# A graph tensor product by sorted buckets: 4.5 instead of 5 slot tiles a bucket in the first of three parts

## The chip, the cores and the metric

The kernel runs on one core of a Trainium2 chip. Its engines work side by side, each in the order of its own queue: PE (matrix products; its weight loads are listed as PEld), DVE (VectorE), ACT (ScalarE), POOL (GpSimd, which here issues the indirect DMAs) and SP (SyncE, which issues the plain DMAs). The metric is device time in microseconds (us), the median of several runs; less is better.

## The reference

A graph has N = 10000 nodes and E = 640000 edges, each with a random source and a random destination. Every node carries 64 channels of 4 numbers, every edge 4 numbers Y and 4 edge features.

```python
np.random.seed(seed)                                   # seed = 0
src = np.random.randint(0, N, size=E); dst = np.random.randint(0, N, size=E)
...
R = silu(edge_feat @ w_rad)                            # (E, 64)
xs = x[src]                                            # (E, 64, 4)
tp = einsum('eci,ef,ifo->eco', xs, Y, cg)
agg = segment_sum(R[:, :, None] * tp, dst, N)          # sum over the edges into a node
out = einsum('ncm,cd->ndm', agg, w_mix)
```

So for each edge a row of x is gathered, scaled per channel by R, combined with Y, and added to its destination. The constant combination with `cg` and `w_mix` is linear and comes last, after the sum over edges.

## The kernel before

**Tiles and parts.** 128 edges are a tile, and E is 5000 tiles. `SPLIT` (L35) cuts them into three parts: 0.3, 0.355 and 0.345 of the tiles (1488, 1776 and 1736). Each part is sorted by destination in two passes and then summed up.

**First sort** (`pass1`, L703). The nodes form 20 groups. Chunks of up to 24 tiles (16 in the first part) are routed so that the edges of a group lie together in the memory array `grp`. PE does the routing with one-hot matrices (L650), which ACT and DVE build (L623, L635, L639); POOL writes each chunk to memory with one indirect DMA (L669). The first part's first sort, and the second sort of its first group, run before any messages; the first sorts of parts two and three are woven into the messages of the part before.

**Second sort** (`pass2`, L804). The groups of a part are sorted the same way into buckets of up to 32 nodes, 15 or 16 to a group and 313 in all, in the memory array `bkt`. Each bucket there has a fixed row of slots: `BT = 17` tiles of 128, of which part k owns `SPLIT[k][1]` (5, 6, 6). Within a bucket a running counter says where the next edge goes. When a part begins, the counter is raised to the first slot of that part (`kc` in `front`, L821), so slots that the part before left free stay empty; when a part has more edges than slots, they run on into the next part's slots. Only the end of the whole row is a limit: a chunk's piece of a bucket that would cross it is sent whole to a spill list behind `bkt` (`tables`, L471: `over`, `sc`, `kov`). A piece has 8 rows of S slots, S being what a chunk can need at most: 35 for a chunk of up to 24 tiles, 12 for the short chunk of 6 tiles that closes each group of the last part.

**Messages** (`messages`, L894). A unit is one bucket in one part. `load_bucket` (L376) brings the slots of a whole group into `pay` with 8 DMAs on SP, one for each of the 8 rows in which a bucket's slots are interleaved. `index` (L915) splits the keys into source and destination. `gather` (L938) issues one indirect DMA on POOL for each tile, 128 rows of x into a buffer `xg` with room for 7 units. `rests`, `spell`, `turn`, `turned`, `radial` and `silu` make R; `products` (L1017, DVE, L1021) multiplies it into `xg`; `spots` (L1005, DVE, L1011 and L1014) makes S, which holds Y in the column of the edge's node within the bucket and zero elsewhere; `sums` (L1023, PE, L1032) adds up `xg` times S over the unit's tiles in one PSUM tile G; `evict` (L1048) takes it out and adds the earlier parts' sum, read back from memory (`fetch`, L1041). In the last part the result is mixed (L1080) and stored (L1092).

The order on PE, DVE and ACT is written out: each step of the loop runs the stages of `quarters` for unit k plus a lead, 5 units for the gathers, 8 for the index, 1 for the products, 0 for the sums. `groups` (L1118) weaves in the two sorts by counts of steps. POOL's and SP's instructions stand in program order on their queues.

**The end** (`overflow`, L1194). After the last unit a loop works off the spill lists, first that of the first sort, then that of the second. A pass takes 5 tiles (`OT`): it loads them (L1241), gathers their rows of x (L1262), computes them directly, and for one tile after the other reads the output rows that it touches (L1281), adds (L1316) and writes them back (L1317). The number of passes is computed on the chip from the length of the list. At last the count of edges seen is compared with E; if it differs, the output is cleared and all edges are done over in the same kind of loop (L1229).

Of the kernel before, what the change touches and what calls it, by code (L numbers as in the profile page):

```python
# [18 lines left out]
F = mybir.dt.float32  # L19
BF = mybir.dt.bfloat16  # L20
I32 = mybir.dt.int32
# [4 lines left out]
P = 128  # L26
# [6 lines left out]
BT = 17  # L33
UT = 6
SPLIT = ((0.3, (5,)), (0.355, (6,)), (0.345, (6,)))  # L35
# [68 lines left out]
class Kernel:  # L104
    def __init__(self, ctx, tc, x, src, dst, Y, ef, w_rad, cg, w_mix, out):
# [18 lines left out]
        assert N <= 1 << 14 and BT == sum(sum(u) for _, u in SPLIT)  # L124
# [27 lines left out]
        for _, u in SPLIT:  # L152
            self.btile.append(self.btile[-1] + sum(u))
# [6 lines left out]
        p.stride = BT * P // p.R + p.S  # L160
# [214 lines left out]

    def load_bucket(self, pay, k, g):  # L376

        p, u = self.p2, sum(SPLIT[k][1])
        nb, o = self.nb(g), g * MB * p.R * p.stride * W
        rows = p.dst.rearrange("s w -> (s w)")[o:o + nb * p.R * p.stride * W].rearrange("(b r q) -> r b q", b=nb, r=p.R)  # L380
        s = P // p.R
        a, z = (t * s * W for t in (self.btile[k], self.btile[k + 1]))
        for r in range(p.R):
            self.nc.sync.dma_start(pay[r * s:(r + 1) * s, :nb, :],
                                   rows[r][:, a:z].rearrange("b (p q) -> p b q", p=s))
# [418 lines left out]
    def pass2(self):  # L804
# [44 lines left out]
        for i, (k, g) in enumerate(self.segs):  # L849
            sizes = self.sizes2(k, g)  # L850
            off = [0] + list(itertools.accumulate(sizes))
            if i not in ready:
                yield from front(i, loads(i) if i % self.NG else [load(k, g)])
            D, Wt, tab, c0 = ready.pop(i)

            side = None
            if i and i + 1 < len(self.segs) and self.segs[i + 1][0] == k and i + 1 not in ready:
                side = front(i + 1, loads(i + 1))
            for said in self.route(ps, lambda c: (D[:, off[c]:off[c + 1]], Wt[:, off[c]:off[c + 1]]), sizes,
                                   lambda c: (tab, c0 + c)):  # L860
                if said == "held":
                    if self.held == ps.key:
                        side = self.go(side)[0]
                    yield said
                    continue
                yield max(said - 1, 1)
                if side is not None:
                    side, at = self.go(side)
                    if at == "held":
                        yield at  # L870
                yield 1
            while side is not None:
                side, at = self.go(side)
                yield at
            n = sum(SPLIT[k][1])
            pay = ph.tile([P, MB * max(sum(u) for _, u in SPLIT) * W], F, name="pay")
            pay = pay[:, :MB * n * W].rearrange("p (b q) -> p b q", b=MB)
            self.load_bucket(pay, k, g)
            self.pay[k, g] = pay
            yield  # L880
# [13 lines left out]
    def messages(self):  # L894

        nc, ph = self.nc, self.ph
        units = [((k, g), j, s) for k, g in self.segs for j in range(self.nb(g)) for s in range(len(SPLIT[k][1]))]
        MT = max(sum(u) for _, u in SPLIT)
# [3 lines left out]
        def quad(k):  # L902

            (p, g), j, s = units[k]
            n0, b, nb = self.grp[g]
            j -= j % 4
            return [(n0 + i * b, min(b, self.N - n0 - i * b)) for i in range(j, min(j + 4, nb))]

        def tiles(k):

            g, j, s = units[k]
            u = SPLIT[g[0]][1]
            return sum(u[:s]), u[s]

        def index(k):  # L915

            g, j, s = units[k]
            if s or j:
                return
            m = self.nb(g[1])  # L920
            ut = sum(SPLIT[g[0]][1])
            key = self.pay[g].rearrange("p b (t w) -> p b t w", w=W)[:, :m, :, 0].bitcast(I32)
            si = ph.tile([P, MB, MT], I32, name="sidx", bufs=2)
            nc.vector.tensor_scalar(si[:, :m, :ut], key, (1 << 14) - 1, None, op0=OP.bitwise_and)
            di = ph.tile([P, MB, MT], I32, name="didx", bufs=2)
            nc.vector.tensor_scalar(di[:, :m, :ut], key, 14, None, op0=OP.logical_shift_right)
            dl = ph.tile([P, MB, MT], F, name="dlc", bufs=2)
            n0, b, _ = self.grp[g[1]]
            nc.vector.tensor_scalar(dl[:, :m, :ut], di[:, :m, :ut], float(TD), None, op0=OP.is_ge)
            got = ph.tile([P, 1], F, name="got")  # L930
            nc.vector.tensor_reduce(got, dl[:, :m, :ut], axis=AX.XY, op=OP.add)
            nc.vector.tensor_tensor(self.seen, self.seen, got, op=OP.add)
            nc.vector.scalar_tensor_tensor(dl[:, :m, :ut], di[:, :m, :ut], -float(TD + n0),
                                           self.bn[b][:, :m].unsqueeze(2).to_broadcast([P, m, ut]),
                                           op0=OP.add, op1=OP.subtract)
            IDX[g] = (si, dl)

        def gather(k):  # L938
            g, j, s = units[k]
            si, t0, ut = IDX[g][0][:, j, :], *tiles(k)  # L940
            xg = XG[k] = ph.tile([P, UT, 256], F, name="xg", bufs=LG + 2)
            for t in range(ut):
                u = t0 + t
                nc.gpsimd.indirect_dma_start(  # L944
                    out=xg[:, t, :], out_offset=None, in_=self.x,
                    in_offset=bass.IndirectOffsetOnAxis(ap=si[:, u:u + 1], axis=0))

        def payload(k):
            g, j, s = units[k]
            t0, ut = tiles(k)  # L950
            return self.pay[g][:, j, t0 * W:(t0 + ut) * W], ut

        def rests(k):
            g, j, s = units[k]
            if j % EB:
                return
            ut = tiles(k)[1]
            b = min(EB, self.nb(g[1]) - j)
            ef = self.pay[g][:, j:j + b].rearrange("p b (t w) -> p (b t) w", w=W)[:, :, 5:9]
            top = lambda t: t.bitcast(BF).rearrange("p t (f h) -> p t f h", h=2)[:, :, :, 1]  # L960
            r = ph.tile([P, 2, EB * UT, 4], F, name="rest", bufs=1)
            n = b * ut
            nc.vector.tensor_tensor(r[:, 0, :n], ef, top(ef), op=OP.subtract)
            nc.vector.tensor_tensor(r[:, 1, :n], r[:, 0, :n], top(r[:, 0, :n]), op=OP.subtract)
            EP[k] = [top(ef), top(r[:, 0, :n]), top(r[:, 1, :n])]

        def spell(k):
            g, j, s = units[k]
            if j % EB:
                return  # L970
            E = ph.tile([P, EB * UT * 36], BF, name="E")
            if tiles(k)[1] < UT:
                n = EP[k][0].shape[1] * 36
                nc.vector.memset(E[:, n:n + 36], 0.0)
# [4 lines left out]
            for i in range(min(EB, self.nb(g[1]) - j)):  # L979
                EQ[k + i] = (E, i * tiles(k)[1] * 36)  # L980
# [12 lines left out]
        def radial(k):  # L993
            ut = payload(k)[1]
# [10 lines left out]
        def spots(k):  # L1005
            g, j, s = units[k]
            pb, ut = payload(k)
            pb = pb.rearrange("p (t w) -> p t w", w=W)
            t0 = tiles(k)[0]
            dl = IDX[g][1][:, j, t0:t0 + ut]  # L1010
# [4 lines left out]
                                    pb[:, :, 1:5].unsqueeze(2).to_broadcast([P, ut, NB, 4]), op=OP.mult)  # L1015

        def products(k):  # L1017
            ut = payload(k)[1]
# [4 lines left out]
        def sums(k):  # L1023
            g, j, s = units[k]
            ut = tiles(k)[1]
            if s == 0:
                GP[g, j] = self.ps.tile([P, 2, NB, 4], F, name="G", tag="G", bufs=1)
            G = GP[g, j]
            V, S = VS.pop(k), SS.pop(k)
            for t in range(ut):  # L1030
                for h in range(2):
                    nc.tensor.matmul(G[:, h].rearrange("p n f -> p (n f)"),  # L1032
                                     V[:, t, 32 * h:32 * h + 32, :].rearrange("p c i -> p (c i)"),
                                     S[:, t].rearrange("p n f -> p (n f)"),
                                     start=(s + t + h == 0), stop=(last(k) and t == ut - 1),
                                     skip_group_check=True)

        def last(k):
            return units[k][2] == len(SPLIT[units[k][0][0]][1]) - 1

        def fetch(k):  # L1041

            g, j, s = units[k]
            if g[0] and s == 0:
# [3 lines left out]
        def evict(k):  # L1048
            g, j, s = units[k]
            if not last(k):  # L1050
                return
# [15 lines left out]
        def full(k):  # L1067
            g, j, s = units[k]
            if g[0] == len(SPLIT) - 1 and last(k) and (j % 4 == 3 or j == self.nb(g[1]) - 1):
# [3 lines left out]
        def mix(k):  # L1073
            g, j, s = units[k]
# [9 lines left out]
        def mixed(k, po):  # L1084
            g, j, s = units[k]
# [32 lines left out]
    def groups(self):  # L1118
# [5 lines left out]
        for k, g in segs:  # L1124
            u += self.nb(g) * len(SPLIT[k][1])
# [263 lines left out]
```

## Time and profile before

| | |
|---|---|
| median of 3 runs | 8055.66 us (8052.32 to 8060.37) |
| profiled execution, its own time: the span | 9825.7 us |
| busy PE, weight loads, DVE, ACT, POOL | 74%, 68%, 66%, 40%, 59% of the span |
| indirect DMAs on POOL: gathers, first sort, second sort | 5321, 240, 260 |
| routing matmuls (L650), matmuls of the sums (L1032) | 20530, 21284 |

A float32 matmul appears as two instructions with two weight loads. Rows of the profile name the line, the engine, the operation, the tile written and the tiles read; `x5` is a count. An indirect DMA's time on POOL is the time to issue it, not that of its data. In a row's brackets stands how long the engine was idle before the instruction and what released it. "Remote" means that the releasing event is not among the recorded instructions, "issue" that nothing recorded was waited for. The profiled execution is longer than the others because it is being recorded.

### The profile page before, as it was taken

The numbers are of one execution on the slowest core, as the hardware profiler recorded it, in microseconds if no ns is written. First come the engines' busy times: TensorE is split into PE (matmuls) and PEld (weight loads), VectorE is DVE, ScalarE is ACT, GpSimd is POOL, SyncE is SP. The second block draws the span as 40 slices with busy tenths as digits, with TensorE's granted clock in tenths as the row PEclk, the third lists the DMA queues.
The fourth block names the chain that finished last, engine by engine and source line by source line (L and its number), as shares of the span: only waits on it lengthen the run. The fifth ranks groups of instructions, "written<-read, shape, count | busy, mean of one in ns | idle before, by whom it ended". The sixth has DMA issues, their size and how long they took to land. (4 is left out here: it accounts for less than half of the span.)

```text
span 9825.7 us, 140823 instructions
## 1 busy us (share of the span) xinstructions
PE 7295.1 (74%) x49703; PEld 6709.1 (68%) x49703; DVE 6455.1 (66%) x10943; ACT 3911.8 (40%) x10964; POOL 5796.5 (59%) x6162
## 2 busy tenths in 40 slices
PE   7968877777776777777777777666776777776765
PEld 6867777777776776766767776666676666666664
DVE  8966777767765766777777776565555565555543
ACT  5754544445543443433434344232232332332321
POOL 4645555555556655555565655666666666666664
PEclk8978888888888888888888888787787888878787
DMA  4323333333333334444444443444433434334332
GB/s 185 109 71 105 105 102 101 99 105 102 107 97 113 109 103 116 114 118 116 115 116 113 123 115 111 127 120 121 113 111 111 115 109 115 111 109 111 103 111 67
DMA packets 680536, 1086.77 MB, mean 111 GB/s; under 512 B 255617, under 2 KB 485099, under 8 KB 673552
## 3 DMA queue, kind: packets, MB, share of 16 engines
q0 software_dynamic: 282224, 774.70, 27.8%
q1 hardware_dynamic: 397600, 303.00, 10.4%
q8 instruction: 395, 6.47, 0.3%
q14 instruction: 317, 2.60, 0.1%
HBM read 855.30 MB, written 222.83 MB: 110 GB/s over the span
## 5 line engine op out<-in xcount | busy, mean ns | idle before, releaser
L944 POOL DMA_INDIRECT xg<-in_x_dram,sidx x5321 | 5067.0, 952 | 3304.7 <-issue 1405.5
L1032 PE MATMUL G<-S,xg 128*128 128x128 f32 x21284 | 3317.3, 320 | 961.2 <-issue 391.9
L1032 PEld LDWEIGHTS G<-S,xg 128*128 128x128 f32 x21284 | 3099.7, 231 | 1070.4 <-issue 481.2
L650 PE MATMUL pr<-X,oh 128*128 128x117 f32 (+15 forms) x20530 | 3037.3, 306 | 694.6 <-issue 424.8
L650 PEld LDWEIGHTS pr<-X,oh 128*128 128x128 f32 x20530 | 2837.2, 214 | 858.9 <-issue 515.0
L1021 DVE TENSOR_TENSOR xg<-xg,pre 128x1536 f32<-128x1536 f32 (+1 forms) x939 | 1556.7, 1658 | 293.2 <-ACT pre L1003 158.9
L639 ACT ACTIVATE oh<-i,row 128x128 f32<-128x128 f32 x5322 | 1653.7, 391 | 81.7 <-remote 29.1
L1003 ACT ACTIVATE pre<-pre 128x384 f32<-128x384 f32 (+1 forms) x939 | 429.9, 458 | 3137.0 <-remote 1191.7
L623 DVE TENSOR_TENSOR X<-dv,Wt 128x1512 f32<-128x1512 f32 (+12 forms) x814 | 1337.0, 1642 | 345.2 <-remote 149.6
L1014 DVE TENSOR_TENSOR S<-dv,pay 128x768 f32<-128x768 f32 (+1 forms) x939 | 857.6, 913 | 140.1 <-remote 70.4
L640 ACT ACTIVATE oh<-oh,ones 128x768 f32<-128x768 f32 (+1 forms) x1000 | 862.8, 863 | 32.2
L1061 DVE TENSOR_TENSOR Gs<-old,G 128x256 f32<-128x256 f32 x313 | 131.6, 421 | 1063.2 <-remote 635.9
L635 DVE TENSOR_TENSOR oh<-dv,row 128x768 f32<-128x768 f32 (+3 forms) x960 | 796.0, 834 | 0.1
L991 ACT ACTIVATE sT<-pre 108x256 bf16<-108x256 bf16 x939 | 353.8, 377 | 800.0 <-remote 475.4
L596 DVE TENSOR_REDUCE pos<-pp 128x24 f32<-128x480 f32 (+9 forms) x500 | 267.4, 535 | 528.5 <-remote 333.3
L987 PE MATMUL pre<-idb,E 128*108 128x128 bf16 x1878 | 297.2, 243 | 341.9 <-DVE xg L1021 130.2
L987 PEld LDWEIGHTS <-E 128*108 128x108 bf16 x1878 | 234.1, 145 | 417.9 <-issue 213.4
L999 PE MATMUL pre<-wr,sT 108*128 108x192 bf16 x1878 | 334.3, 261 | 223.1 <-ACT sT L991 137.7
L669 POOL DMA_INDIRECT bkt<-rt,idx x260 | 259.5, 998 | 312.7 <-ACT rt L662 146.8
L1061 DVE TENSOR_TENSOR Gp<-old,G 128x256 f32<-128x256 f32 x313 | 130.8, 418 | 476.8 <-remote 324.5
L999 PEld LDWEIGHTS <-sT 108*128 108x128 bf16 x1878 | 185.6, 108 | 306.8 <-ACT sT L991 155.3
L669 POOL DMA_INDIRECT grp<-rt,idx x240 | 276.7, 1153 | 174.0 <-issue 51.3
(304 smaller groups left out, 4598.7 us busy)
## 6 DMA issues: line engine op xcount, KB each, us to landing
xg<-in_x_dram,sidx POOLq DMA_INDIRECT x5321
sums<-Gp SPq DMA_DIRECT2D x626, 128.0 KB
old<-sums SPq DMA_DIRECT2D x626, 128.0 KB
bkt<-z SPq DMA_DIRECT2D x26, 1024.0 KB
grp<-z SPq DMA_DIRECT2D x23, 1024.0 KB
pay<-bkt SPq DMA_DIRECT2D x208, 54.0 KB
out_dram<-ot SPq DMA_DIRECT2D x69, 128.0 KB
ys<-in_Y_dram SPq DMA_DIRECT2D x65, 96.0 KB
```

The costliest lines, as they stand in the source:

```text
L623: eng.tensor_tensor(X[:, b:e], msk[:, b:e].unsqueeze(3).to_broadcast([P, e - b, w, W]), CH[c][1][:, a + b:a + e, :].unsqueeze(2).to_broadc ...
L635: nc.vector.tensor_tensor(oh[:, :v, :], self.v128.unsqueeze(1).to_broadcast([P, v, P]), row[:, a:a + v].unsqueeze(2).to_broadcast([P, v, P ...
L639: nc.scalar.activation(oh[:, u], self.i128[:, :oh.shape[2]], AF.Square, bias=row[:, a + u:a + u + 1], scale=-1.0)
L640: nc.scalar.activation(oh[:, v:m], oh[:, v:m], AF.Relu, bias=self.ones[:, 0:1], scale=-2.0)
L650: nc.tensor.matmul(PR[c][:, ps.lo[t] * W:ps.hi[t] * W], oh[:, u, :], Xs[u], start=(t == 0), stop=(t == sizes[c] - 1), skip_group_check=True)
L669: nc.gpsimd.indirect_dma_start(out=ps.dst, out_offset=bass.IndirectOffsetOnAxis(ap=idx[:Q, i:i + 1], axis=0), in_=RT.pop(c), in_offset=None)
L944: nc.gpsimd.indirect_dma_start(out=xg[:, t, :], out_offset=None, in_=self.x, in_offset=bass.IndirectOffsetOnAxis(ap=si[:, u:u + 1], axis=0))
L987: nc.tensor.transpose(to[:108, h * P:(h + 1) * P], E[:, o + h * 108:o + h * 108 + 108], self.idb)
L999: nc.tensor.matmul(R[:, h * 192:h * 192 + n * 64], sT[:n * 36, h * P:(h + 1) * P], self.wr[:n * 36, :n * 64], start=True, stop=True)
L1014: nc.vector.tensor_tensor(S[:, :ut], self.eq[:, :ut].unsqueeze(3).to_broadcast([P, ut, NB, 4]), pb[:, :, 1:5].unsqueeze(2).to_broadcast([P ...
L1021: nc.vector.tensor_tensor(V, V, R.unsqueeze(3).to_broadcast([P, ut, 64, 4]), op=OP.mult)
L1032: nc.tensor.matmul(G[:, h].rearrange("p n f -> p (n f)"), V[:, t, 32 * h:32 * h + 32, :].rearrange("p c i -> p (c i)"), S[:, t].rearrange( ...
```

## The change

In the first part a bucket gets 4.5 tiles of slots: two neighbouring buckets (2i and 2i + 1) share one tile, the first taking its rows 0 to 63, the second its rows 64 to 127. The shares of the edges become 0.2875, 0.355 and 0.3575 (1440, 1776 and 1784 tiles), and a bucket's row of slots becomes 16.5 tiles long. With this:

- `share` says for bucket j of part k which tiles it gathers (5 for the first of a pair, with the shared tile; 4 for the second) and over which it sums (5 for both).
- `load_bucket` fetches, in the first part, own tiles and half tiles separately, for even and odd buckets: 32 DMAs a group, and one more that zeroes the unused half where the number of buckets is odd.
- The tiles of a group lie in `pay` one behind the other. `index` computes the local destination once for each of the two kinds of bucket, and twice for a shared tile, so that S is zero for the other bucket's rows.
- `sums` of an odd bucket also reads the shared tile from the buffer of the unit before, which is kept until then.
- A unit is now always a whole bucket (the third index `s`, which was always 0, goes).

```diff
-BT = 17
-SPLIT = ((0.3, (5,)), (0.355, (6,)), (0.345, (6,)))
+SPLIT = ((0.2875, 4.5), (0.355, 6), (0.3575, 6))
+BT = sum(u for _, u in SPLIT)
...
+    def share(self, k, j):
+
+        n = SPLIT[k][1]
+        m = int(n)
+        if m == n:
+            return j * m, m, j * m, m
+        at = j // 2 * (2 * m + 1)
+        return (at + m + 1, m, at + m, m + 1) if j % 2 else (at, m + 1, at, m + 1)
+
+    def tiles(self, k, g):
+
+        a, n, _, _ = self.share(k, self.nb(g) - 1)
+        return a + n
...
+        to = pay[:, :MB // 2 * (2 * m + 1) * W].rearrange("p (b q) -> p b q", b=MB // 2)
+        if nb % 2:
+            self.nc.sync.dma_start(to[P // 2:, nb // 2, m * W:(m + 1) * W], self.zr[:P // 2, :W])
+        c = a + m * s * W
+        for h in range(2):
+            b = (nb + 1 - h) // 2
+            for r in range(p.R):
+                row = rows[r][h::2, :]
+                q = h * (m + 1) * W
+                self.nc.sync.dma_start(to[r * s:(r + 1) * s, :b, q:q + m * W],
+                                       row[:, a:c].rearrange("b (p q) -> p b q", p=s))
+                i = h * P // 2 + r * s // 2
+                self.nc.sync.dma_start(to[i:i + s // 2, :b, m * W:(m + 1) * W],
+                                       row[:, c:z].rearrange("b (p q) -> p b q", p=s // 2))
...
         def gather(k):
-            g, j, s = units[k]
-            si, t0, ut = IDX[g][0][:, j, :], *tiles(k)
+            g, j = units[k]
+            t0, ut = tiles(k)
+            si = IDX[g][0]
...
         def sums(k):
-            g, j, s = units[k]
-            ut = tiles(k)[1]
-            if s == 0:
-                GP[g, j] = self.ps.tile([P, 2, NB, 4], F, name="G", tag="G", bufs=1)
-            G = GP[g, j]
-            V, S = VS.pop(k), SS.pop(k)
+            g, j = units[k]
+            t0, _, a, ut = self.share(g[0], j)
+            G = GP[g, j] = self.ps.tile([P, 2, NB, 4], F, name="G", tag="G", bufs=1)
+            S = SS.pop(k)
             for t in range(ut):
+                V, u = (VS[k], a + t - t0) if a + t >= t0 else (VS[k - 1], a + t - tiles(k - 1)[0])
                 for h in range(2):
                     nc.tensor.matmul(G[:, h].rearrange("p n f -> p (n f)"),
-                                     V[:, t, 32 * h:32 * h + 32, :].rearrange("p c i -> p (c i)"),
+                                     V[:, u, 32 * h:32 * h + 32, :].rearrange("p c i -> p (c i)"),
                                      S[:, t].rearrange("p n f -> p (n f)"),
-                                     start=(s + t + h == 0), stop=(last(k) and t == ut - 1),
+                                     start=(t + h == 0), stop=(t == ut - 1),
                                      skip_group_check=True)
+            VS.pop(k - 1, None)
```

139 lines of the change are left out of this document (70 added, 69 removed).

## The prediction

> **What bounds the kernel now.** I read the span cut at the kernel's own seams: the opening sort (to the first gather), the messages of the three parts, and the end. The columns are the stretch, its length, then busy us and instructions of PE, PEld, DVE, ACT, POOL, the granted clock, DMA share and GB/s.
>
> ```profile
> 0.00:598.00 598.00, 494.73 (x3557) 435.33 (x3558) 518.98 (x1281) 390.11 (x1204) 305.89 (x420) 0.89 0.36 128
> 598.00:3503.00 2905.00, 2235.99 (x15569) 2068.61 (x15569) 2041.88 (x3478) 1413.59 (x4017) 1660.39 (x1727) 0.83 0.36 104
> 3503.00:6757.00 3254.00, 2422.16 (x16590) 2234.03 (x16590) 2244.25 (x3452) 1255.37 (x3419) 1941.57 (x2029) 0.83 0.41 117
> 6757.00:9721.00 2964.00, 2105.73 (x13797) 1942.19 (x13797) 1614.41 (x2598) 844.09 (x2295) 1871.60 (x1969) 0.81 0.39 111
> ...
> 9755.00:9806.00 51.00, 18.07 (x65) 12.86 (x65) 22.84 (x105) 6.65 (x25) 15.03 (x15) 0.60 0.08 20
> ...
> sum 9826.00, PE 7295.15 PEld 6709.14 DVE 6455.07 ACT 3911.82 POOL 5796.49; mean PE 1042.16 PEld 958.45 DVE 922.15 ACT 558.83 POOL 828.07
> ```
>
> No engine is full, so next I looked at how POOL spends its time (timeline, then POOL's waits in the first part: total, times, longest).
>
> ```profile
> 9645.02 0.95 POOL L944 DMA_INDIRECT xg<-in_x_dram,sidx  x1 [0.30 <-issue]
> 9646.27 0.94 POOL L944 DMA_INDIRECT xg<-in_x_dram,sidx  x1 [0.30 <-issue]
> 9647.51 0.95 POOL L944 DMA_INDIRECT xg<-in_x_dram,sidx  x1 [0.30 <-issue]
> ```
> ```profile
> POOL xg L944 <- issue: 402.4, 1287, 5.2
> POOL xg L944 <- PE G L1032: 367.8, 97, 14.1
> ```
>
> A gather shows 0.95 us of work, but the next starts 1.25 us after it when nothing holds it. At that pitch POOL needs 1727 x 1.25 = 2159, 2029 x 1.25 = 2536 and 1969 x 1.25 = 2461 us in the three message parts. The second wait is POOL out of gather buffers: PE has not finished the sums of an older unit.
>
> The profiled execution's own time is its span, 9825.7 us; nothing around it is recorded. The runs' median is 8055.66, so profiling stretched it by 1770 us. I spread that over the 49703 matmuls of the page, 35.6 ns each. It is an assumption, but one with a test: it leaves 2905 - 554 = 2351, 3254 - 591 = 2663 and 2964 - 491 = 2473 us. The last is within 0.5% of POOL's 2461. So I take the last part as paced by POOL's queue, the second nearly so (2536 of 2663), and the first as shared: POOL 2159 of 2351 (0.918), DVE 2042 of 2351 (0.869). The terms below are unstretched differences; to the profile's own time they add almost alike, as matmuls hardly change (about 10,150 us).
>
> **The change, part by part.** All counts follow from the split and the kernel's formulas.
>
> *Gathers.* A pair of buckets fetches 9 tiles instead of 10. The 20 groups have 16 (13 of them) or 15 buckets (7): 13 x 72 + 7 x 68 = 1412 gathers in part one, against 1565. 153 fewer at 1.25 us is 191 us of POOL's queue. The sums are untouched: each bucket still multiplies 5 tiles, the shared one twice with different rows live. DVE's S tiles (L1014) stay too. Its products shrink in 153 units by one tile:
>
> ```profile
> L1021 DVE TENSOR_TENSOR xg<-xg,pre 128x1536 f32<-128x1536 f32 x626 | 1093.3, 1747 | 152.8 <-DMA xg<-in_x_dram,sidx 57.9 <-ACT pre L1003 56.0 <-issue 20.3
> L1021 DVE TENSOR_TENSOR xg<-xg,pre 128x1280 f32<-128x1280 f32 x313 | 463.4, 1480 | 140.4 <-ACT pre L1003 102.9 <-DMA xg<-in_x_dram,sidx 20.1 <-issue 11.7
> L623 DVE TENSOR_TENSOR X<-dv,Wt 128x1512 f32<-128x1512 f32 (+9 forms) x327 | 555.0, 1697 | 196.7 <-remote 89.6 <-PE pr L650 43.9 <-PE pre L987 14.5
> L635 DVE TENSOR_TENSOR oh<-dv,row 128x768 f32<-128x768 f32 (+3 forms) x326 | 262.7, 813 | 0.0
> ```
>
> 153 x (1747 - 1480) ns = 41 us. The smaller share also takes 39 tiles (1575 to 1536) from part one's second sort; spread and one-hots (the last two rows, in that part's window) are some 2.5 us for a piece of 10 to 12 tiles, with the small operations about 0.3 us a tile: 12 us. DVE falls from 2042 to 1989. If POOL held the whole path the gain is 191; if nothing but DVE did, at its present share, 2351 - 1989 / 0.869 = 62; if PE's unchanged sums did, 0. I take **-110**, between DVE's and POOL's answers and nearer DVE's: POOL's need falls to 1968, below DVE's, and a shared tile now keeps its buffer one unit longer (until the next bucket's sums), which lengthens the wait of POOL on L1032 quoted above.
>
> [...]
>
> *Loads of a group's slots.* Part one issues 32 or 33 small transfers for a group instead of 8, on SP.
>
> ```profile
> 1248.13 4.00 SPq L384 DMA_DIRECT2D pay<-bkt  x8
> ```
> ```profile
> 1349.81 0.22 DVE L924 TENSOR_SCALAR sidx<-pay 128x80 int32<-128x80 int32 x1
> ```
>
> At 0.5 us each they take 16.5 us, and DVE reads them 98 us after the last issue: hidden, 0. Behind them on SP wait the stores of the partial sums, which have two buffers. A store 16.5 us late plus 2 us to land would hold the eviction two units on, due after 15 us (2351 / 313 = 7.5 each): at worst 3.5 us for 19 groups, 67 us. I keep that only in the range.
>
> *Other shares.* The opening sort has 90 chunks instead of 93: at most 598 / 93 = 6.4 us each, less the constants and the first group's own sort; **-13** (-19 to -10). The last part's first sort has 75 chunks for 73 (two stores, 2.5 us of POOL; 48 tiles, 15 us of DVE), beside part two's messages: **+10** (0 to 25). The last part's second sort grows by 60 tiles, 19 us of DVE where DVE stands at 1614 of 2473: **+5** (0 to 19).
>
> *Capacity.* This decides. A bucket of 32 nodes receives 640000 x 32 / 10000 = 2048 edges on average, with a spread of 45. Its slots fall from 17 x 128 = 2176 to 16.5 x 128 = 2112, from 2.8 spreads of room to 1.4, before the slots that stay empty where a part ends short of its line. A bucket's piece of a chunk that crosses the end goes whole to a spill list: 8 x 35 = 280 slots, or 8 x 12 = 96 for the short last chunk. The closing loop works that list off 5 tiles (640 slots) a pass. The edges are drawn with a fixed seed, so I followed them through the placement rules. Before: 6 pieces of 96, 576 slots, one pass. After: 42 pieces of 96 and 5 of 280, 5432 slots, 8.5, so **nine passes**. The profile agrees on the one pass of before (five tiles loaded in all), and shows what it costs:
>
> ```profile
> opay<-bkt SPq DMA_DIRECT2D x5, 4.5 KB
> ```
> ```profile
> 9755.20 2.53 SPq L1241 DMA_DIRECT2D opay<-bkt  x5
> ...
> 9779.00 0.42 DVE L1316 TENSOR_TENSOR ocur<-ocur,oout 128x256 f32<-128x256 f32 x1
> ...
> 9797.31 1.02 POOL L1317 DMA_INDIRECT out_dram<-ocur,odi  x1 [2.31 <-DVE ocur L1316]
> 9799.84 1.03 POOL L1281 DMA_INDIRECT ocur<-out_dram,odi  x1 [1.50 <-DMA out_dram<-ocur,odi]
> 9802.50 0.42 DVE L1316 TENSOR_TENSOR ocur<-ocur,oout 128x256 f32<-128x256 f32 x1 [5.46 <-DMA ocur<-out_dram,odi]
> 9803.21 1.02 POOL L1317 DMA_INDIRECT out_dram<-ocur,odi  x1 [2.34 <-DVE ocur L1316]
> 9806.90 0.09 PEld L1217 LDWEIGHTS cp<-ones,seen 128*1 128x1 f32 x2 [23.28 <-issue]
> ```
> ```profile
> 9803.21 2.21 DMA out_dram<-ocur,odi
> ```
>
> From the first load to the first instruction after the loop: 51.7 us. Within it each tile reads rows of the output, adds and writes them back before the next may read, 5.9 us a tile; the passes are serial and nothing else runs. 8 more passes are **+414**. From below: the 65 matmuls' stretch off and no time to go round, 8 x (50.2 - 2.3) = 383, with 50.2 from the first load to the last landing (9803.21 + 2.21). From above: 5.5 us to go round, the time from DVE's last instruction before the spill loop of the first sort (which makes no pass) to PE's next after it:
>
> ```profile
> 9745.88 0.27 DVE L1223 MEMSET zo<- 16x256 f32 x1
> 9751.67 0.34 PEld L1203 LDWEIGHTS cp<-kov,ones 1*80 1x80 f32 x2 [11.02 <-issue]
> ```
>
> That gives 8 x 55.7 = 446.
>
> *Sum.* -110 - 13 + 10 + 5 + 414 = +306: 9825.7 becomes some 10,150 with the added matmuls' stretch, and 8055.66 becomes **8362 us**. All ends together: 8055.66 + 383 - 191 - 19 = 8229 and 8055.66 + 446 + 67 - 10 + 25 + 19 = 8603.
>
> **The rivals.**
> *The messages give nothing back.* PE and DVE already pace part one, and the gathers saved only turn POOL's work into waiting. For it: POOL's 368 us of waiting on L1032. Against: the 0.918. 8055.66 + 414 - 13 + 15 = 8472. [...]
> *POOL was the whole path.* All 191 come back: 8055.66 + 414 - 191 - 13 + 3 = 8269. For it: the fit of part three; against: DVE's 0.869 in part one.
> *Faster.* The spill does not grow, because the edges timed are not the ones I followed or a rule of placement was read wrongly. Then -110 - 13 + 15 = -108: 7948 with one pass. This decides below 108 / 51.7 = 2.1 extra passes, that is up to three passes, 1920 slots, 20 short pieces. For it: the count is mine, and no row shows it but the one pass of before. Against: it gave that pass right, and the room of 1.4 spreads alone leaves a twelfth of 313 buckets over the end.
> *The change loses edges.* The kernel counts the edges that it has seen and, if any is missing, does all 5000 tiles again, 1000 passes: over 50 ms. The two halves of a shared tile are disjoint rows and each is counted once, so 1%.
>
> **How the numbers follow.** Forecast 0.73 (its own range 8285 to 8455), nothing back 0.12, POOL's whole path 0.08, faster 0.05, something else 0.02. Two runs of this kernel can be told apart from about 0.2% (16 us). Slower holds the first three: 0.93; faster 0.05; the same 0.02 (two extra passes). The range, 8262 to 8478, takes in both slower rivals' times and leaves out the far ends.
>
> **What would show it.** In the changed profile the spill load (L1241's line) should be there 45 times, five for each pass, with the end after the last unit some 410 us longer. The gathers should number 5168. Part one's stretch should be shorter by about 110, with POOL's waits on the sums a larger share of it; shorter by 190 or unchanged decides between the two slower rivals. DVE's first read of a group's slots should still wait for nothing. The prediction is wrong if the loop runs fewer than seven times or a pass costs under 45 us.

## The result, and the profile after

The changed kernel takes **8422.5 us** (8419.84 to 8430.0, 4 runs) against 8058.0 us of the kernel before beside it (8052.32 to 8062.69, 4 runs). The ratio is 1.0458, 95% interval 1.0445 to 1.0471: slower by 364.5 us.

Executions of the kernel before fell into two kinds, about 8,050 us at a granted clock of 0.90 and 9,800 to 9,950 us at 0.82, and the only record at hand for the forecast (9825.7 us) is of the second kind, while the record of after is of the first (span 8428.2 in a run of 8430.0 us). It is therefore set against e1 below, the kernel before recorded once more: that execution took 8052.4 us, with a span of 8050.6, so a recorded execution can have the usual length. The statement ahead of the prediction that the profiled execution is longer because it is being recorded is not borne out.

The span of the kernel before in e1's record, cut at the same seams as in the prediction: to the first gather, the messages of the three parts, the end. The columns are the stretch, its length, busy us and instructions of PE, PEld, DVE, ACT, POOL, the granted clock, DMA share and GB/s.

```profile
0.00:594.00 594.00, 488.32 (x3557) 430.00 (x3558) 517.45 (x1281) 390.19 (x1204) 310.10 (x421) 0.90 0.37 129
594.00:2899.00 2305.00, 1970.87 (x15589) 1865.34 (x15589) 2038.80 (x3482) 1411.19 (x4025) 1661.88 (x1726) 0.92 0.46 130
2899.00:5473.00 2574.00, 2132.95 (x16703) 2016.10 (x16702) 2245.59 (x3474) 1263.81 (x3429) 1947.24 (x2029) 0.92 0.52 148
5473.00:7950.00 2477.00, 1927.07 (x13739) 1805.90 (x13739) 1592.47 (x2579) 844.07 (x2281) 1877.35 (x1968) 0.87 0.46 132
7950.00:8050.00 100.00, 29.14 (x120) 22.10 (x118) 29.32 (x129) 7.05 (x26) 18.11 (x19) 0.61 0.07 16
```

The same view of the changed kernel:

```profile
0.00:592.50 592.50, 477.16 (x3446) 417.43 (x3447) 501.22 (x1254) 378.15 (x1168) 301.00 (x412) 0.89 0.36 127
592.50:2868.70 2276.20, 1974.53 (x15541) 1848.58 (x15541) 1986.87 (x3497) 1399.89 (x4035) 1517.27 (x1576) 0.92 0.44 123
2868.70:5446.80 2578.10, 2153.77 (x16794) 2040.56 (x16793) 2254.75 (x3484) 1269.26 (x3454) 1944.50 (x2030) 0.92 0.52 148
5446.80:7919.60 2472.80, 1936.90 (x13840) 1816.63 (x13840) 1608.58 (x2561) 843.87 (x2281) 1873.37 (x1968) 0.87 0.46 132
7919.60:8428.00 508.40, 177.75 (x646) 129.02 (x645) 222.85 (x1009) 60.26 (x226) 137.54 (x139) 0.60 0.08 20
```

The difference of the two records, stretch by stretch, beside the terms of the forecast:

| stretch | before (e1) | after | difference | forecast |
|---|---|---|---|---|
| opening sort, to the first gather | 594.0 | 592.5 | -1.5 | -13 |
| messages of part one | 2305.0 | 2276.2 | -29 | -110 |
| messages of part two | 2574.0 | 2578.1 | +4 | +10 |
| messages of part three | 2477.0 | 2472.8 | -4 | +5 |
| last gather to the end | 100.6 | 508.6 | +408 | +414 |
| span | 8050.6 | 8428.2 | +377.6 | +306 |

The loss stands in the last stretch. Groups of the spill load, in the kernel before (e1) and then in the changed one (count; shortest, median and longest in ns; first and last start in us):

```profile
L1241 SPq DMA_DIRECT2D opay<-bkt x5: 333/333/379, 7980.1 to 7982.3; - x5
```
```profile
L1271 SPq DMA_DIRECT2D opay<-bkt x45: 332/333/376, 7949.6 to 8371.2; - x45
```

45 loads instead of 5 are nine passes instead of one, as forecast, and 408 / 8 = 51.0 us is the price of a pass. PE, DVE, ACT and POOL are busy for 35%, 44%, 12% and 27% of the last stretch: no engine is near full there, as the steps of a pass wait for one another: at one tile's end DVE's add (L1346, at 8052.58 us) had waited 5.49 us for the output rows read, and the write back on POOL (L1347) 2.34 us for that add.

The gain in part one is small: most of POOL's freed time came back as waiting. POOL's groups in part one, before (e1) and after: count, busy us and mean ns, then POOL's idle time just before them and what ended it.

```profile
L944 POOL DMA_INDIRECT xg<-in_x_dram,sidx x1565 | 1496.7, 956 | 587.3 <-issue 416.1 <-PE G L1032 88.9 <-PE pre L987 11.7
L669 POOL DMA_INDIRECT bkt<-rt,idx x83 | 83.7, 1008 | 39.0 <-issue 20.1 <-ACT sT L991 4.5 <-ACT Wt L770 3.8
L669 POOL DMA_INDIRECT grp<-rt,idx x78 | 81.5, 1045 | 24.7 <-issue 18.6 <-ACT pre L1003 1.5 <-DMA Wt<-grp 1.2
```
```profile
L978 POOL DMA_INDIRECT xg<-in_x_dram,sidx x1413 | 1352.3, 957 | 636.7 <-issue 366.6 <-PE G L1066 112.4 <-DVE dv L648 34.6
L700 POOL DMA_INDIRECT bkt<-rt,idx x84 | 83.3, 992 | 109.0 <-ACT rt L693 26.9 <-issue 15.9 <-ACT sT L1027 12.9
L700 POOL DMA_INDIRECT grp<-rt,idx x79 | 82.6, 1046 | 29.1 <-issue 13.4 <-ACT rt L691 5.2 <-ACT pre L1039 2.1
```

POOL issues 1576 indirect DMAs instead of 1726. At the pitch of 1.25 us (two gathers in a row start at 1245.67 and 1246.92 us in the changed kernel as well, 0.95 us of work and 0.30 idle) that frees 188 us. Its idle time before the three groups is 587.3 + 39.0 + 24.7 = 651 us before and 636.7 + 109.0 + 29.1 = 775 us after. Of this, 0.30 us an instruction belongs to the pitch (518 and 473 us), and the wait of the first gather (8 and 16 us) lies before the stretch, so the true waits rise from 125 to 286 us. That is 161 of the 188 us, spread over the sums (buffers not yet free), DVE's steps and ACT's copies that the stores need. This says where POOL's time went, not which engine held it up.

What the gathers themselves hold up is DVE's products. Their row in part one, before (e1) and after:

```profile
L1021 DVE TENSOR_TENSOR xg<-xg,pre 128x1280 f32<-128x1280 f32 x309 | 457.2, 1480 | 73.6 <-DMA xg<-in_x_dram,sidx 41.1 <-ACT pre L1003 28.2 <-ACT Gp L1063 3.2
```
```profile
L1056 DVE TENSOR_TENSOR xg<-xg,pre 128x1280 f32<-128x1280 f32 (+1 forms) x309 | 416.9, 1349 | 65.6 <-DMA xg<-in_x_dram,sidx 30.9 <-ACT pre L1039 30.6 <-ACT oh L671 1.7
```

In the whole of part one the products waited 41.1 us for gathered rows before the change, and 30.9 after it. There was little for an earlier gather to save at this place.

The change also adds a wait. A group's 32 slot loads stand on SP ahead of the stores of the partial sums, and an eviction (L1093) waits until the store from its buffer has landed. The last slot load of a group, the store behind it and the eviction that waits, 2.08 us after the store's issue began, in the changed kernel:

```profile
1246.62 0.35 SPq L415 DMA_DIRECT2D pay<-bkt  x1
...
1247.07 0.34 SPq L1095 DMA_DIRECT2D sums<-Gp  x1
...
1249.15 0.38 ACT L1093 ACTIVATE Gp<-G 128x256 f32<-128x256 f32 x1 [4.49 <-DMA sums<-Gp]
```

All evictions of part one, before (e1) and after:

```profile
L1063 ACT ACTIVATE Gp<-G 128x256 f32<-128x256 f32 x307 | 116.1, 378 | 330.6 <-PE G L1032 313.9 <-DMA sums<-Gp 13.9 <-DMA pay<-bkt 1.9
```
```profile
L1093 ACT ACTIVATE Gp<-G 128x256 f32<-128x256 f32 x307 | 115.8, 377 | 340.9 <-PE G L1066 285.6 <-DMA sums<-Gp 48.2 <-PE pre L1035 5.3
```

They waited for these stores twice before (13.9 us in all) and nine times after (48.2 us).

### The profile page after: what moved, and what is told of

The parts are those of the page before. It is cut to its first block, busy times and chain, and to the rows that moved or that the text cites. A ratio compares the mean times of both kernels' runs of the same rounds, so it can differ in the third digit from the quotient of the medians.

```text
span 8428.2 us, 143963 instructions
## 1 busy us (share of the span) xinstructions
PE 6720.1 (80%) x50262; PEld 6252.2 (74%) x50262; DVE 6574.3 (78%) x11803; ACT 3951.4 (47%) x11164; POOL 5773.7 (69%) x6122
## 5 line engine op out<-in xcount | busy, mean ns | idle before, releaser
L978 POOL DMA_INDIRECT xg<-in_x_dram,sidx x5168 | 4927.0, 953 | 1788.9 <-issue 1393.8
L1066 PE MATMUL G<-S,xg 128*128 128x128 f32 x21284 | 2983.0, 304 | 60.9 <-DVE Gp L1091 25.0
L1066 PEld LDWEIGHTS G<-S,xg 128*128 128x128 f32 x21284 | 2833.1, 217 | 110.0 <-DVE Gp L1091 52.8
L681 PE MATMUL pr<-X,oh 128*128 128x108 f32 (+14 forms) x20572 | 2689.7, 290 | 277.5 <-DVE oh L666 165.6
L681 PEld LDWEIGHTS pr<-X,oh 128*128 128x128 f32 x20572 | 2565.3, 200 | 366.6 <-DVE oh L666 176.2
L1056 DVE TENSOR_TENSOR xg<-xg,pre 128x1536 f32<-128x1536 f32 (+2 forms) x939 | 1516.9, 1615 | 850.2 <-DMA xg<-in_x_dram,sidx 537.3
L654 DVE TENSOR_TENSOR X<-dv,Wt 128x1512 f32<-128x1512 f32 (+11 forms) x818 | 1345.9, 1645 | 117.6 <-PE pr L681 71.5
L1039 ACT ACTIVATE pre<-pre 128x384 f32<-128x384 f32 (+2 forms) x939 | 422.0, 449 | 1567.9 <-PE pre L1035 1249.3
L691 ACT ACTIVATE rt<-pr 120x252 f32<-120x252 f32 (+10 forms) x499 | 202.3, 407 | 529.1 <-DMA bkt<-rt,idx 361.7
L1046 DVE TENSOR_TENSOR dv<-dv,dlc 128x192 f32<-128x192 f32 (+1 forms) x939 | 328.5, 350 | 11.2
```

The lines of the kernel that those rows point to most:

```text
L654: eng.tensor_tensor(X[:, b:e], msk[:, b:e].unsqueeze(3).to_broadcast([P, e - b, w, W]), CH[c][1][:, a + b:a + e, :].unsqueeze(2).to_broadc ...
L681: nc.tensor.matmul(PR[c][:, ps.lo[t] * W:ps.hi[t] * W], oh[:, u, :], Xs[u], start=(t == 0), stop=(t == sizes[c] - 1), skip_group_check=True)
L978: nc.gpsimd.indirect_dma_start(out=xg[:, t, :], out_offset=None, in_=self.x, in_offset=bass.IndirectOffsetOnAxis(ap=si[:, u:u + 1], axis=0))
L1056: nc.vector.tensor_tensor(V, V, R.unsqueeze(3).to_broadcast([P, ut, 64, 4]), op=OP.mult)
L1066: nc.tensor.matmul(G[:, h].rearrange("p n f -> p (n f)"), V[:, u, 32 * h:32 * h + 32, :].rearrange("p c i -> p (c i)"), S[:, t].rearrange( ...
```

## The experiments

The first four ran on one chip beside the kernel before (8053.8 us, 13 runs). The other two groups ran on two other chips, on which before takes 9846 and 9950 us; their times are compared only within their own group.

**e1: the kernel before again, no edit.** It was run for a record of an execution of the usual length.

> The kernel before, unchanged, for a second record of where its time goes. Theory A (the first part's messages are shared between POOL and DVE, and the change gave back little there): the span is near the runs' 8058 us, the opening about 595, the last part's messages about 2473 as after the change, the second part's about 2575 and the first part's about 2310, some 35 us longer than the 2276 of the changed kernel. Rival B (the prediction's split, and the gain of 110 was had but spent elsewhere): first part 2351 or more, second part 2663, opening about 470.

Measured: 8052.6 us, ratio 1.0001 (0.9991 to 1.0012), span 8050.6. The rows are above, and the lengths are those of theory A. This record shows no stretch by recording, and the prediction's lengths for three of the four stretches were wrong (see below).

**e2: one pass.** The change, with the closing loop of the second sort fixed at one pass; the edges of its other eight passes are missing from the output, and the two loops that would do lost edges over are held at zero.

```diff
-            nc.vector.tensor_scalar(ni, count, 1.0 / m, (m - 0.5) / m - 0.5, op0=OP.mult, op1=OP.add)
+            cut = (0.0, 1.0) if ps is self.p2 else (1.0 / m, (m - 0.5) / m - 0.5)
+            nc.vector.tensor_scalar(ni, count, *cut, op0=OP.mult, op1=OP.add)
...
-            nc.vector.tensor_scalar(ni, lost, float(self.N // 16), None, op0=OP.mult)
+            nc.vector.tensor_scalar(ni, lost, 0.0, None, op0=OP.mult)
...
-            nc.vector.tensor_scalar(nj, lost, float(self.NT // OT), None, op0=OP.mult)
+            nc.vector.tensor_scalar(nj, lost, 0.0, None, op0=OP.mult)
```

> The changed kernel, whose loop over the spill list of the second sort always makes one pass, and whose comparison of the edges seen leads to nothing; the edges of the other eight passes are left out of the output. Theory A (the loop is what the change costs): 8 passes of 52.0 us less than the changed kernel, 8422 - 416 = 8006 us, which is 52 us or 0.6% under the kernel before. Rival B (the time went into the messages, and passes after the first are cheap): 8300 us or more. Rival C (the messages gained the predicted 110): 7945 us.

Measured: 8005.4 us, ratio 0.9943 (0.9927 to 0.9960), where theory A had 8006. Its opening and part one, in the stretch view:

```profile
0.00:593.50 593.50, 479.50 (x3446) 419.39 (x3447) 502.66 (x1254) 378.73 (x1168) 298.65 (x411) 0.88 0.36 127
593.50:2864.60 2271.10, 1977.05 (x15541) 1851.54 (x15540) 1986.41 (x3497) 1399.73 (x4035) 1515.91 (x1576) 0.92 0.44 123
```

8422.5 - 8005.4 = 417 us are the eight passes, 52.1 each. Everything else that the change does is worth 8053.8 - 8005.4 = 48 us, 34 of it in part one (2305.0 to 2271.1). This is the part that had been put at 108.

**e3 and e4: each half of the change alone.** e3 keeps five whole tiles a bucket and takes the new shares; e4 keeps the old shares and lets neighbours share a tile. e3 leaves the row at 17 tiles but brings more edges into its last third; e4 shortens the row to 16.5. Followed through the placement rules as in the prediction, both spill to a count of six passes.

```diff
-SPLIT = ((0.2875, 4.5), (0.355, 6), (0.3575, 6))
+SPLIT = ((0.2875, 5), (0.355, 6), (0.3575, 6))     # e3
+SPLIT = ((0.3, 4.5), (0.355, 6), (0.345, 6))       # e4
```

> The new shares of the edges alone, with five whole tiles of slots in the first part. Followed through the placement rules the spill list has 30 pieces of 96 and 2 of 280 slots, 3440 in all: 6 passes. Theory A: 8058 + 5 x 52 = 8318, less 6 for the shorter opening, plus 0 to 10 for the larger last part: 8312 to 8322 us. Rival B (the shared tiles alone make the spill grow): 8050 to 8065 us.

> The shared tiles alone, with the old shares of the edges. By the placement rules 25 pieces of 96 and 4 of 280 slots, 3520: 6 passes. Theory A (gain of 35 to 60 us in the first part's messages): 8058 + 260 - 35 to 60 = 8258 to 8283 us. The prediction's gain of 110 would give 8208 us; a gain of all 191 us of POOL's queue 8127 us. Rival B (the shares alone make the spill grow): below 8058 us.

Measured: e3 8292.8 us, ratio 1.0301 (1.0284 to 1.0319); e4 8294.1 us, ratio 1.0306 (1.0289 to 1.0323). Opening and part one of e3, and its spill loads:

```profile
0.00:580.60 580.60, 474.29 (x3446) 417.28 (x3447) 503.36 (x1254) 378.25 (x1168) 299.41 (x411) 0.89 0.37 131
580.60:2877.30 2296.70, 1959.70 (x15523) 1854.84 (x15523) 2029.88 (x3482) 1413.52 (x4034) 1663.71 (x1726) 0.92 0.46 131
```
```profile
L1271 SPq DMA_DIRECT2D opay<-bkt x30: 332/333/386, 7962.4 to 8232.3; - x30
```

The same of e4:

```profile
0.00:599.90 599.90, 486.28 (x3557) 425.87 (x3558) 516.90 (x1281) 390.07 (x1204) 311.80 (x421) 0.90 0.36 127
599.90:2888.30 2288.40, 1993.64 (x15589) 1865.29 (x15589) 1996.09 (x3502) 1396.94 (x4025) 1517.66 (x1575) 0.92 0.44 122
```
```profile
L1271 SPq DMA_DIRECT2D opay<-bkt x30: 332/333/380, 7967.9 to 8233.0; - x30
```

30 loads are six passes in each. e3 is 239 us over before and e4 240 us, and five more passes at 52.1 are 260, so each half gains about 20 us beside its passes. Both expected times were missed by a little: e3 is 19 us below its 8312 to 8322, and e4 11 us above its 8258 to 8283. In part one the shares give 8 us (2305.0 to 2296.7) and the pairs 17 (to 2288.4); together they give 29 to 34. The pairs alone take 151 indirect DMAs off POOL (1726 to 1575, 189 us), about as many as the whole change does. They also bring the 32 slot loads a group that stand ahead of the late stores: for these ACT waits 48.2 us in the changed kernel and 55.5 in e2, both with 32 loads, against 13.9 in e1, with 8.

The opening shows a cost that the prediction had put at nothing. In e3 it shortens by 13.4 us, the -13 of the forecast, but in e4 it grows by 5.9 and in the changed kernel nothing is left of the 13. Timeline from the last store of the opening sort to the first gather, before (e1) and after:

```profile
585.05 0.95 POOL L669 DMA_INDIRECT bkt<-rt,idx  x1 [4.00 <-ACT rt L662]
587.55 3.96 SPq L384 DMA_DIRECT2D pay<-bkt  x8
593.45 0.23 DVE L924 TENSOR_SCALAR sidx<-pay 128x80 int32<-128x80 int32 x1 [14.26 <-DMA pay<-bkt]
...
593.95 0.98 POOL L944 DMA_INDIRECT xg<-in_x_dram,sidx  x1 [7.95 <-DVE didx L926]
```
```profile
575.65 0.95 POOL L700 DMA_INDIRECT bkt<-rt,idx  x1 [3.99 <-ACT rt L693]
578.17 0.34 SPq L412 DMA_DIRECT2D pay<-bkt  x1
...
590.09 0.33 SPq L415 DMA_DIRECT2D pay<-bkt  x1
591.98 0.22 DVE L951 TENSOR_SCALAR sidx<-pay 128x72 int32<-128x72 int32 x1 [22.29 <-DMA pay<-bkt]
...
592.48 0.99 POOL L978 DMA_INDIRECT xg<-in_x_dram,sidx  x1 [15.87 <-DVE didx L953]
```

From the store to the first gather it takes 8.9 us before and 16.8 after. The first group has no older unit to hide behind: its 32 loads, 0.37 us apart, stand open before the first gather, and take 8 us of the 13. The other 4 us between e3 and the changed kernel lie ahead of the last store and are not explained.

**e5 to e8: which engine paces part one once POOL is relieved.** Two one-hots a piece go from DVE to ACT in the woven sorts of all three parts, on before (e5) and on the one-pass kernel (e6); the sums of part one leave out two of a bucket's tiles, on the one-pass kernel (e7) and with the shift (e8). The edges of the tiles left out, and those of the passes left out, are missing from the outputs of e6, e7 and e8.

```diff
-            self.rt_bufs, self.ls, self.act, self.spare = 3, 4, 6, 0
+            self.rt_bufs, self.ls, self.act, self.spare = 3, 4, 8, 0     # e5, e6, e8
...
-            for t in range(ut):
+            few = ut if g[0] else ut - 2                                 # e7, e8
+            for t in range(few):
...
-                                     start=(t + h == 0), stop=(t == ut - 1),
+                                     start=(t + h == 0), stop=(t == few - 1),
```

> The kernel before; in the woven second sort of part one ScalarE makes eight one-hots of each piece instead of six, and VectorE four instead of six. By the rows of the one-pass run (VectorE's one-hots 259.5 us for 328 pieces, ScalarE's 606.7 us for 1968 squares and 306.8 us for 328 relus) VectorE loses a third, about 87 us of its 2039 in part one (2305 us long), and ScalarE gains about 200 + 90 us on its 1411. Theory A, VectorE paces part one: part one shortens by 60 to 90 us, time about 7965 to 7995. Theory B, GpSimd's queue paces it (1726 issues by 1.25 us = 2158 us of 2305): no more than 20 us. Theory C, TensorE (1971 us busy) and its in-order waits for ScalarE pace it: nothing gained, and with ScalarE at about 1700 us up to 60 us lost.

> The one-pass run (pairs and shares of the change, spill loop of the second sort at one pass, the edges of its other passes left out of the output; 8005.4 us, part one 2271 us) with the same shift of one-hots from VectorE to ScalarE. GpSimd's issues are 1574 by 1.25 us = 1969 us here, so it leaves room. Theory A, VectorE (1985 us) took over the pace when GpSimd was relieved: part one falls by 60 to 90 us, time 7915 to 7945. Theory C, TensorE (1975 us) and the order of waits: no gain, 0 to 60 us lost, 8005 to 8065.

> The one-pass run; the sums of part one multiply only all but the last two of a bucket's slot tiles (the others' edges are left out of the output). TensorE loses 2 of 5 sums there, about 0.4 x 837 = 330 us of its 1975 in part one; no other engine's work changes. Theory A, VectorE paces part one: 0 to 30 us shorter, 7975 to 8005. Theory C, TensorE paces it: 100 us shorter or more, up to the other engines' 1985 us, so 7750 to 7905.

> Both at once: fewer sums in part one and two one-hots a piece shifted from VectorE to ScalarE, on the one-pass run; edges left out as there. If one engine paces part one, this run equals the better of the two alone (theory A: 7915 to 7945; theory C: 7750 to 7905). If neither alone helps and both together do, two engines pace it together, each waiting for the other in turn. If this too stays within 20 us of 8005, what paces it is the order of the woven steps or the slot buffers, not the work of TensorE or VectorE.

Measured, against before at 9845.7 us: e5 9944.2 us, ratio 1.0111 (1.0084 to 1.0138); e6 10137.3, 1.0293 (1.0273 to 1.0313); e7 9908.4, 1.0062 (1.0040 to 1.0084); e8 9990.7, 1.0139 (1.0101 to 1.0176). The expected times had been worked out for a chip on which before takes 8053 us, so only their order can be judged here. Theory A (DVE alone paces part one) gets no support on this chip: taking some 87 us off DVE gained nothing in e5. What was not expected at all is that e6 is slower than e5, although its POOL has 152 fewer DMAs to issue in part one and its closing loop is no longer. For that the one-pass kernel without the shift was missing, hence the next four.

**e9 to e12: the same on one chip with the one-pass kernel beside them.** e9 is e2, e10 is e6, e11 is e7 and e12 is e5, each unchanged and with what it leaves out.

> The one-pass run again (edges of the spill loop's other passes left out of the output), so that it stands beside the three that follow on one chip. On a chip on which before takes about 8053 us (granted clock 0.90): ratio 0.994 as measured. [...]

> The one-pass run with two one-hots a piece shifted from VectorE to ScalarE, beside e9 on the same chip. At clock 0.90: theory A (VectorE paces part one) 60 to 90 us below e9; theory C (TensorE and the order of waits) 0 to 60 us above it. At 0.82: above e9 by 50 to 110 us (before lost 98 us by the shift there).

> The one-pass run with two of a bucket's slot tiles left out of the sums of part one (their edges are left out of the output), beside e9. At clock 0.90: theory A 0 to 30 us below e9; theory C 100 us or more below it. At 0.82: 100 to 200 us below e9 by either, since TensorE's gaps bound every part there.

> The kernel before with the same shift of one-hots. At clock 0.90: theory A (VectorE paces part one of before) 60 to 90 us faster than before, ratio about 0.990; theory B (GpSimd's queue) within 20 us; theory C 0 to 60 us slower. At 0.82: ratio 1.011 as measured.

Measured, against before at 9950.4 us: e9 10247.8 us, ratio 1.0292 (1.0275 to 1.0309); e10 10339.9, 1.0384 (1.0367 to 1.0401); e11 10051.1, 1.0099 (1.0082 to 1.0115); e12 10040.9, 1.0091 (1.0072 to 1.0110). Their part one in the stretch view, in the order e9, e10, e11, e12:

```profile
592.00:3785.60 3193.60, 2359.47 (x15533) 2153.76 (x15533) 1994.85 (x3502) 1408.11 (x4035) 1516.99 (x1576) 0.80 0.31 88
```
```profile
598.50:3843.20 3244.70, 2379.49 (x15532) 2177.25 (x15532) 1910.08 (x3502) 1666.37 (x4691) 1519.67 (x1575) 0.79 0.31 86
```
```profile
593.00:3600.80 3007.80, 2114.49 (x13078) 1914.25 (x13078) 1994.88 (x3502) 1402.65 (x4035) 1516.24 (x1576) 0.76 0.33 93
```
```profile
596.00:3563.00 2967.00, 2253.65 (x15569) 2085.56 (x15569) 1953.97 (x3478) 1668.09 (x4669) 1658.96 (x1726) 0.83 0.36 101
```

Three things follow for a chip of this kind. Moving DVE's work to ACT does not help (e10 against e9: DVE 85 us less busy, ACT 258 more, part one 51 us longer), so DVE alone doesn't pace part one; whether relief of DVE without the load on ACT would help was not tested. TensorE's work does count (e11 against e9: PE 245 us less busy, part one 186 us shorter). And the pairs and shares, which save a little at 0.92, here cost a great deal: with the shift in both, part one goes from 2967.0 (e12) to 3244.7 us (e10), while POOL has 151 DMAs fewer. That the one-pass kernel without the shift is slow too (e9, 1.0292, where e2 had 0.9943) says that the loss doesn't come from the shift. The author's estimate for e9 in that case, 1.01 to 1.02, had the direction but not the size; those for e10, e11 and e12 on such a chip came out. That TensorE's gaps bound every part there, the reason given for e11, is not shown.

Where the 278 us are can partly be read. PE's two large groups in part one of e12, then of e10: count, busy us and mean ns, then PE's idle time before them.

```profile
L650 PE MATMUL pr<-X,oh 128*128 128x108 f32 (+12 forms) x7164 | 1079.9, 311 | 283.2 <-issue 118.2 <-ACT rt L660 93.1 <-ACT oh L640 31.2
L1032 PE MATMUL G<-S,xg 128*128 128x128 f32 x6140 | 969.9, 319 | 209.6 <-issue 138.5 <-ACT Gp L1063 66.4 <-DMA xg<-in_x_dram,sidx 1.5
```
```profile
L681 PE MATMUL pr<-X,oh 128*128 128x108 f32 (+14 forms) x7116 | 1128.1, 321 | 330.8 <-issue 167.3 <-ACT rt L691 97.8 <-ACT oh L671 30.7
L1066 PE MATMUL G<-S,xg 128*128 128x128 f32 x6147 | 1006.3, 327 | 203.3 <-issue 137.2 <-ACT Gp L1093 60.9 <-DMA xg<-in_x_dram,sidx 2.9
```

PE is busy 126 us longer for as many matmuls (8 to 10 ns more each, at a clock of 0.79 for 0.83) and idle for the other 152. Why the pairs and shares bring this isn't settled. On the chip of the first four runs the question which of PE, DVE and the written order paces part one was not tested, since both later groups came to other chips.

No kernel of these beats the one before and still sums all edges.

## Why the prediction was right, and where it was off

The forecast was 8362 us, and 8422.5 was measured, inside its range of 8262 to 8478. The cause that it named, more passes of the closing loop, is the one that the runs show. That the time fell into the range is in part luck: the range took in the times of both slower rivals, and the term for part one was nearly four times too large.

*Capacity: right, in count and price.* Nine passes were forecast and 45 loads are there. The +414 was measured as +408 (records) and 417 (runs of after and e2).

*Gathers: right in count, and the term of -110 is the one that was mis-sized.* 5168 gathers were forecast and 5168 are there. Part one gave -29 us in the changed kernel and -34 in e2. The prediction put the answer between DVE's (-62) and POOL's (-191). It lies below both: with the lengths of e1, DVE at its share would have given 2305 - 1986.9 / (2038.8 / 2305) = 59 us, PE at its unchanged work 0, and the measured gain is about half way between those two. The step that failed is the choice of the bounds: POOL, at 0.918 of part one, was taken to hold a share of the path, and the 0 that stood there for PE's unchanged sums was left out of the weighing. POOL's share was even 2158 / 2305 = 0.936, and still 161 of the 188 us freed came back as POOL's own waiting; the products had waited only 41.1 us for its gathers. The prediction's own row of the 128x1280 products had 20.1 us for this wait and could have told. The 29 us are not POOL's alone either: DVE's work in part one fell by 52 us with the same change, and no run separates the two. That DVE (0.88) and PE (0.86) pace part one by waiting for one another in their written order fits these rows, but no run on this chip tests it. Of the two rivals on this term, "gives nothing back" (8472) was nearer in its mechanism than "POOL was the whole path" (8269); the forecast lay between them.

The measured -29 is nearer to the 0 at the lower end of that weighing than to -110. The busy shares in e1's record point the same way for part one, where DVE is busy for 0.88 and POOL for 0.72. In part two DVE's share is the higher one as well (0.87 against 0.76), though POOL's 2029 DMAs need 2536 of 2574 us at their pitch; in part three POOL's busy share, 0.76, understates the 2460 of 2477 us that its 1968 DMAs need.

*The stretch of the record: wrong.* The prediction took the 1770 us between record and runs for the cost of recording and spread it over the matmuls, 35.6 ns each. The record of e1 has 594, 2305, 2574 and 2477 us where this gave 471, 2351, 2663 and 2473. Only part three fits, and that one fit had been the test. It made part two look less bound by POOL than it is, and its forecast of about 10,150 us for the profile after was off by 1,700. Its effect on the sum is small, since the terms were differences: with e1's lengths DVE's answer is 59 instead of 62.

*Loads of a group's slots: the 0 was wrong in two places.* It was argued from a row of a later group. DVE's read did wait for nothing in the later groups, as forecast (of the 60 reads at L951 only the first waited for its slots, 22.3 us), but the first group's loads stand before the first gather and cost 8 us, the larger part of why the opening term of -13 came out as -1.5; with whole tiles (e3) it was -13.4. And the stores behind the loads of later groups came late, which the prediction had weighed but kept only in its range (at worst 67 us): ACT waited 34 us longer for them. How much of that reaches the span is not shown; PE's waits for these evictions rose from 11.9 to 17.9 us.

*Part two +10 and the last part's second sort +5:* measured +4 and -4, nothing either way. POOL's queue nearly fills those stretches, which would explain it; no run tests that.

*The sum.* The -110 gave back 81 us too little, the opening 12, and the two small terms and the loop came out 21 lower: 306 + 81 + 12 - 21 = 378, the 377.6 of the records.

## What to carry to other kernels

Before an engine is freed, look at how long the others wait for what it makes. Here POOL stood at 0.94 of a stretch, but its consumer waited only 41 us for it, and 188 us less of work brought 29. The rest came back as waits on the freed engine. Ask too what small transfers will stand in front of on their queue: the slot loads were early enough for their own reader and still delayed the stores behind them. Before slots are made fewer, count what overflows and what one round of the overflow path costs: here four passes at 52 us would already outweigh all that the 188 us off POOL could bring. And before a record is scaled to a run of another length, find out what kind of execution it is of; one stretch that happens to fit is no test.

## What the runs showed of the hardware beyond what was expected

The same program takes 8053.8, 9845.7 and 9950.4 us on three chips, at granted clocks of 0.90, 0.82 and 0.82. VectorE's work is the same in e1 and in the record quoted in the prediction (2039 and 2042 us in part one), and so is the opening sort (594 and 598 us). The messages take the whole difference: part one lasts 2305 us in e1 and 2905 in that record. PE's two large groups in part one of e1:

```profile
L650 PE MATMUL pr<-X,oh 128*128 128x108 f32 (+12 forms) x7164 | 945.2, 291 | 95.6 <-ACT rt L660 53.1 <-DVE oh L635 40.5 <-ACT pre L1003 0.8
L1032 PE MATMUL G<-S,xg 128*128 128x128 f32 x6158 | 844.7, 298 | 11.9 <-ACT Gp L1063 11.9
```

The same groups in that record:

```profile
L650 PE MATMUL pr<-X,oh 128*128 128x108 f32 (+12 forms) x7164 | 1062.0, 309 | 210.0 <-issue 104.7 <-ACT rt L660 48.5 <-DVE oh L635 39.1
L1032 PE MATMUL G<-S,xg 128*128 128x128 f32 x6140 | 970.1, 318 | 200.4 <-issue 147.6 <-ACT Gp L1063 43.2 <-DMA xg<-in_x_dram,sidx 6.4
```

In part one of e1 these two rows name no wait put down to "issue", that is, to nothing that the profile shows; in the longer record the two groups wait 105 and 148 us for it, and 410 us instead of 108 in all. What sets the chips apart is not shown. With this the sign of an edit can turn: the one-pass kernel has the ratio 0.9943 on the one chip and 1.0292 on another, both well outside their intervals.

In three of the records the order of PE's idle time in part one is the reverse of that of its granted clock: 334 us and 0.92 in e1, 713 and 0.83 in e12, 865 and 0.79 in e10. The rows don't show which comes first, the gaps or the low clock. Nor can the mean clock be read as a time where the work differs: e11, with fewer sums, has a lower clock than e9 (0.76 and 0.80) and a shorter part one (3007.8 and 3193.6 us).
